# The first feed-forward unit split in two, and first blocks loaded in 1 KB runs from two queues

## The chip, the cores and the metric

The kernel runs on one NeuronCore of a Trainium2 chip. The metric is the device time of one execution, in microseconds (us). Before the change it is 294.58 us, the median of three runs (294.3 to 295.22). The profile is one execution recorded by the hardware profiler, with a span of 293.9 us.

Five engines work side by side, each on its own instruction queue: TensorE (PE, matrix products, with PEld for loading its stationary operand), VectorE (DVE), ScalarE (ACT), GpSimd (POOL) and SyncE (SP, which only issues transfers). Sixteen DMA engines move data. SP, ScalarE and GpSimd can start transfers.

## The reference

There are 4 batches, 8 heads, 768 rows and 64 columns per head. Attention is causal and restricted: keys form chunks of 32 rows, and each query attends to at most six chunks, chosen by an upper bound on its scores.

```python
ub = np.sum(np.maximum(q * k_min, q * k_max), axis=-1)     # per query and chunk
top_chunks = np.argsort(ub, axis=-1)[..., -top_k:]         # top_k = 6
scores = scale * np.matmul(q, k.transpose(0, 1, 3, 2))
mask = sel & (pos[:, None] >= pos[None, :])
attn = softmax(where(mask, scores, -1e9)); x = attn @ v
```

Then a gated feed-forward runs over all 3072 rows, with the heads side by side as 512 columns:

```python
gate = 1.0 / (1.0 + np.exp(-(x @ w_gate)))     # w_gate, w_val: 512 x 1536
val = x @ w_val
return gate * val @ w_out                      # w_out: 1536 x 512
```

The first 128 rows of a batch see only four chunks, so nothing is chosen for them: plain causal attention is enough.

## The kernel before, in words

The rows are cut into blocks of 128. A *first block* is block 0 of a batch; batches are numbered 0 to 3. Blocks are grouped into *units* of three blocks (384 rows), and each unit goes through the feed-forward together. Unit 0 holds the first blocks of batches 0, 1 and 2. Unit 2 holds two blocks of batch 0 and the first block of batch 3. The other six units hold three ordinary blocks each.

*First blocks* (`first`, L807 and on). SP loads k and q in two halves of four heads each (L742) and v whole (L737). The descriptors are runs of 64 numbers, 256 bytes, since a row of one head is 64 numbers. PE turns k and q (tiles kfT, qfT, L815) with four transposes of 128x128 each against a 32-bit identity, and they are cast to 16 bits (kf, qf). Then come scores (scf, L852), exponentials on ScalarE (attf, L857), the causal mask on GpSimd (L859), the product with v (pvf, L866), the division by the sum (rzf L872, xf L874), and the turn back (xpsf, L881) into xT, the input of the feed-forward. For batch 0 alone the keys of the first block are also kept in hk and their chunk minima and maxima in kcr, for later queries.

*Ordinary units.* For each, keys and queries are turned (`keys_wide`, `queries_wide`, tiles kn, kT, kt, qn, qT, qf, for units 1 and 2; `keys_blocks`, `turn_queries`, for later batches, on VectorE), the bounds are computed on PE with 32-bit operands (ub, L1002) and chunks are chosen on VectorE (`choose`: ubn, mx, ap, apt). Chosen chunks are encoded in the unused half of hq and hk, so that one product gives masked scores (`attend`: sc L1063, att L1074, mask L1080, pv L1096, x L1115, xps L1123).

*Feed-forward* (`ffn`, L1131 and on). For each of 12 parts of 128 hidden columns: four products for the gate (g, L1146), tanh on ScalarE (gate, L1154), four products for the value (v, L1146), and their combination on VectorE (hg, L1158). Then 12 products for each 128 rows (o, L1168), scaled (osb, L1177) and stored by SP (L1180). The tile name v_u is the value product; wg, wv and wo are the weights.

*Weights* are loaded by GpSimd with a cast from 32 to 16 bits, each of the three matrices in three transfers (L718, L719, L724). wg and wv are each cut by hidden columns; a third serves four parts of the feed-forward.

*Order.* The program lists operations with engines they may run on, estimated durations, priorities and dependencies. A planner (`Plan.walk`) walks through time and picks for each engine the ready operation of best priority. The priorities are shifted by the table NUDGES, and the assumed landings of transfers come from LANDS. The result is a fixed order for every engine; on the chip each instruction then waits only for what it needs. Buffers come from pools of fixed size, chosen by the planner ("np", "hg", "xt", "qm", "ubn" and others).

The loads of first blocks 0 to 2 come first on SP, then k and q of unit 1 (kq_u), then v. The first block of batch 3 is loaded and treated in the middle of unit 2. Weight transfers 2 and 3 and wo wait in the order for the masks of batch 2's first block.

The softmax here doesn't subtract the row's maximum and nothing guards it: scores larger than these inputs give would overflow.

## Time and profile before

| | |
|---|---|
| median of three runs | 294.58 us |
| span of the profile | 293.9 us |
| PE busy | 278.2 us, 95% |
| ACT, DVE, POOL busy | 195.8, 189.2, 92.5 us |
| bytes moved by DMA | 32.69 MB in 123233 packets, 111424 of them under 512 B |
| SP issue of a first-block transfer | 0.5 us |
| first transposes of first block 0, 1, 2 | 4.95, 7.86, 10.18 to 13.24 us |

The page gives busy time by engine, then the span in 40 slices with the tenths of each slice that an engine is busy, the clock granted to TensorE and the rate of transfers. Views of the trace list instructions in order of time, the wait before each and what ended it, and the busy time of engines in chosen stretches. Successive PE instructions overlap at their ends, so their pace is read from start to start. The chain of work that ended last goes from the transfers of q through those of wo (9% of the span) to PE, which makes up 78% of it.

### The profile page before, as it was taken

To read this page: it belongs to the slowest core of one execution; us is meant where nothing else is said; L and a number is where in the kernel's file an instruction comes from. 1 tells how busy PE (TensorE), PEld (TensorE's weight loads), DVE (VectorE), ACT (ScalarE), POOL (GpSimd) and SP (SyncE) were. 2 spreads that over 40 slices of the span, in tenths; PEclk is the share of its full clock that TensorE was granted. 3 is DMA by queue.
4 is the path that set the end of the run, shared out by engine and by line. 5 is a ranking of instruction groups with operands and counts; after the bars stand their busy time and mean duration, and the time that the engine had idled before them with its cause. 6 is when DMAs were issued, how large, how long until landed. Compare 5 with 4: busy or idle time off the path is not lost.

```text
span 293.9 us, 6954 instructions
## 1 busy us (share of the span) xinstructions
PE 278.2 (95%) x2656; PEld 176.7 (60%) x2656; DVE 189.2 (64%) x560; ACT 195.8 (67%) x398; POOL 92.5 (31%) x162
## 2 busy tenths in 40 slices
PE   2879998999989999999999999999999999999994
PEld 2645555767664566556666667676565557655651
DVE  8375883996999289999999899654134124432420
ACT  7674757977984879458889898886563466323321
POOL 6681314933652337013326954213000011000000
PEclk9977999999999999999999999999999999999999
DMA  7999999999967999399997300001100110011002
GB/s 165 218 249 216 197 197 235 220 146 166 184 100 90 203 188 184 67 215 152 142 210 145 111 3 3 0 2 39 71 2 1 50 60 0 2 38 71 0 15 95
DMA packets 123233, 32.69 MB, mean 111 GB/s; under 512 B 111424, under 2 KB 120128, under 8 KB 123200
## 3 DMA queue, kind: packets, MB, share of 16 engines
q1 hardware_dynamic: 118448, 27.53, 53.1%
q0 software_dynamic: 4752, 4.72, 9.5%
q8 instruction: 21, 0.34, 0.5%
q14 instruction: 12, 0.10, 0.1%
HBM read 30.67 MB, written 6.29 MB: 126 GB/s over the span
## 4 chain that ended last, share of the span: by engine, by line
PE 78%; DMA 10%; DVE 4%; SPq 2%; POOL 2%; ACT 1%; issue 1%; ACTq 0%; DVEq 0%
PE o_u L1168 20%; PE v_u L1146 18%; PE g_u L1146 18%; PE sc_u L1063 11%; DMA wo<-in_moe_w_out_dram 9%; PE pv_u L1096 6%; PE ube_u L1002 2%; SPq L742 2%; PE xps_u L1123 2%; DMA qf<-in_q_dram 1%; DVE qf_u L969 1%; DVE kcr L787 1%; DVE kt L953 1%; ACT attf L857 1%; PE qfT L815 1%
## 5 line engine op out<-in xcount | busy, mean ns | idle before, releaser
L1074 ACT ACTIVATE att_u<-sc_u 128x512 f16<-128x512 f32 (+3 forms) x184 | 88.0, 549 | 13.9 <-PE sc_u L1063 13.1
L1158 DVE SCALAR_TENSOR_TENSOR hg_u<-gate_u,v_u 128x384 f16<-128x384 f16 x96 | 51.8, 544 | 53.8 <-PE v_u L1146 37.0
L1146 PE MATMUL g_u<-xT_u,wg 128*128 128x384 f16 x384 | 79.3, 330 | 0.0
L1146 PE MATMUL v_u<-xT_u,wv 128*128 128x384 f16 x384 | 78.8, 328 | 0.3 <-DMA wv<-in_moe_w_val_dram 0.3
L1154 ACT ACTIVATE gate_u<-g_u 128x384 f16<-128x384 f32 x96 | 47.6, 495 | 39.1 <-DVE hg_u L1158 21.5
L1168 PE MATMUL o_u<-wo,hg_u 128*128 128x512 f16 x288 | 68.0, 379 | 1.1 <-DMA wo<-in_moe_w_out_dram 1.1
L1080 POOL TENSOR_SCALAR_AFFINE_SELECT att_u<-att_u 128x384 f16<-128x384 f16 (+1 forms) x56 | 28.4, 512 | 99.0 <-ACT att_u L1074 98.2
L1146 PEld LDWEIGHTS <-wv 128*128 128x128 f16 x384 | 36.8, 98 | 23.5 <-issue 0.8
L1146 PEld LDWEIGHTS <-wg 128*128 128x128 f16 x384 | 36.5, 99 | 21.8 <-issue 1.5
L1168 PEld LDWEIGHTS <-hg_u 128*128 128x128 f16 x288 | 27.1, 98 | 28.7 <-issue 1.5
L1177 ACT ACTIVATE osb_u<-o_u 128x512 f32<-128x512 f32 x20 | 12.1, 603 | 26.7 <-PE o_u L1168 25.0
L1096 PEld LDWEIGHTS <-att_u 128*128 128x128 f16 x640 | 25.5, 98 | 4.7
L1096 PE MATMUL pv_u<-v,att_u 128*128 128x65 f16 x640 | 28.0, 193 | 0.0
L1063 PE MATMUL sc_u<-hqo,hko 128*128 128x128 f16 (+2 forms) x220 | 27.8, 243 | 0.1
L1063 PE MATMUL sc_u<-hqe,hke 128*128 128x128 f16 (+2 forms) x220 | 27.1, 243 | 0.2 <-ACT att_u L1074 0.2
L1063 PEld LDWEIGHTS <-hke 128*128 128x128 f16 x220 | 16.8, 98 | 5.7 <-issue 1.2
L779 POOL CAST v<-v 128x512 f16<-128x512 f32 x23 | 13.9, 619 | 19.2 <-DMA v<-in_v_dram 18.9
L1063 PEld LDWEIGHTS <-hko 128*128 128x128 f16 x220 | 16.3, 98 | 4.8 <-issue 0.2
L576 DVE COPY xT_u<-xps_u 128x384 f16<-128x384 f16 (+1 forms) x17 | 5.7, 338 | 14.4 <-PE xps_u L1123 14.3
L1115 DVE TENSOR_TENSOR x_u<-pv_u,rz_u 128x384 f16<-128x384 f32 (+1 forms) x28 | 14.5, 523 | 0.4
L1025 DVE MAX8 mx_u<-ubn_u 128x8 f32<-128x8 f32 (+16 forms) x152 | 12.4, 156 | 0.1
L787 DVE TRANSPOSE_TENSOR_REDUCE kcr<-k 128x24 f32<-128x768 f32 x12 | 11.2, 941 | 0.8 <-DMA k<-in_k_dram 0.8
(119 smaller groups left out, 306.9 us busy)
## 6 DMA issues: line engine op xcount, KB each, us to landing
out_dram<-osb_u SPq DMA_DIRECT2D x24, 256.0 KB, 2.4
v<-in_v_dram SPq DMA_DIRECT2D x23, 256.0 KB, 5.0
k<-in_k_dram SPq DMA_DIRECT2D x12, 384.0 KB, 6.1
q<-in_q_dram SPq DMA_DIRECT2D x12, 384.0 KB, 6.8
wg<-in_moe_w_gate_dram POOLq DMA_DIRECT2D x3, 512.0 KB, 10.2
wv<-in_moe_w_val_dram POOLq DMA_DIRECT2D x3, 512.0 KB, 12.8
wo<-in_moe_w_out_dram POOLq DMA_DIRECT2D x3, 512.0 KB, 23.3
kf<-in_k_dram SPq DMA_DIRECT2D x8, 128.0 KB, 3.6
```

Source lines behind the costliest of these rows:

```text
L779: plan.add(f"v16_{b}_{ib}", {POOL: pool(H * D)}, lambda e: nc.gpsimd.tensor_copy(v16[b % 2][:, ib, :, 0:D], at(t)), reads=[t], writes=[("v ...
L787: plan.add(f"kx{m}_{name}_{p}", {DVE: dve(size)}, lambda e, m=m, op=op: nc.vector.tensor_reduce(out=outs[m](), in_=src(), op=op, axis=AX.X ...
L1025: nc.vector.max(at(mx)[:, e_, j, :], at(ubn)[:, e_, j, 0:max(8, u.seen[j])])
L1063: nc.tensor.matmul(at(t)[:, o:o + 128 * m], hk[b % 2][e_][:, p, 128 * jb:128 * jb + 128], hq[u.side][e_][:, p, 128 * x:128 * (x + m)], sta ...
L1074: plan.add(f"exp_{u.name}_{h}_{y}", {ACT: act(n)}, lambda e, t=t, att=att, b0=b0, n=n: nc.scalar.activation(at(att)[:, b0:b0 + n], at(t), ...
L1080: nc.gpsimd.affine_select(out=dv, in_=dv, compare_op=ALU.is_ge, fill=0.0, base=0, pattern=[[0, u.m], [1, 128]], channel_multiplier=-1)
L1096: nc.tensor.matmul(at(pv)[:, last, x, :], at(att)[:, c:c + 128], v16[b % 2][:, jb, h, :], start=(jb == 0), stop=(jb == ib))
L1115: plan.add(f"x_{u.name}_{p}", {DVE: dve(u.t)}, lambda e: nc.vector.tensor_tensor(at(x_).rearrange("p a (e d) -> p e a d", e=2), at(pv)[:, ...
L1146: nc.tensor.matmul(at(t), w16[:, c, 128 * fb:128 * fb + 128], at(u.xt)[:, c, :], start=(c == 0), stop=(c == 3))
L1154: plan.add(f"tanh_{u.name}_{fb}", {ACT: act(T)}, lambda e, g=g, gate=gate: nc.scalar.activation(at(gate), at(g), AF.Tanh, scale=0.5), read ...
L1158: plan.add(f"hg_{u.name}_{fb}", {DVE: dve(T)}, lambda e, w_=w_, gate=gate, hg=hg: nc.vector.scalar_tensor_tensor(at(hg), at(gate), 1.0, at ...
L1168: nc.tensor.matmul(at(o), at(hgs[fc])[:, 128 * tb:128 * tb + 128], wo16[:, fc, :], start=(fc == 0), stop=(fc == NFB - 1))
```

## The change

Five things change together.

1. Unit 0 keeps only the first blocks of batches 0 and 1 (256 rows). A new unit 8, also of 256 rows, holds the first blocks of batches 2 and 3. Unit 2 becomes 256 rows. Both feed-forwards of the start do four gate products before their first four value products. The weights are still cut in three, but keyed by hidden part.
2. k and q of first blocks are read as runs of four rows, 1 KB, which puts four rows of a head on one partition. All four blocks are loaded at the start; k by SP, q by ScalarE, v by either. Turning them takes eight ordinary 32-bit products of 64 outputs instead of four transposes, and the cast puts rows back in order.
3. Unneeded space is lent: 16-bit k and q, the exponentials and v of first blocks live in parts of hk, hq and v16 that come into use later; these later uses wait for the products pvf.
4. Products of the identity with itself (warm) are added at places where PE is expected idle, to keep its clock up.
5. The order is planned anew, with a table HOLDS that gives some operations an earliest time. ubn shares the buffer of qm.

The core of the diff:

```diff
-        Unit(0, [], [(0, 0), (1, 1), (2, 2)]),
+        Unit(0, [], [(0, 0), (1, 1)]),
-        Unit(2, [(0, 4), (0, 5)], [(3, 2)]),
+        Unit(2, [(0, 4), (0, 5)]),
+        Unit(8, [], [(2, 0), (3, 1)]),
...
-                for e_ in range(2):
-                    plan.add(f"{n}f{e_}_{b}", {SP: (450, 450)}, lambda e, t=t[n], src=src, e_=e_: nc.sync.dma_start(
-                        at(t).rearrange("s (p e) d -> s e p d", e=2)[:, e_], heads(src, b, e_)[:, 0:128].rearrange("p s d -> s p d")),
-                        writes=[(t[n], e_)], prio=prio + 0.1 * j, dma=(1125 if (b, n, e_) == (0, "k", 1) else 575, 256))
+                for g in range(2):
+                    plan.add(f"{n}f{g}_{b}", {(SP, ACT)[j]: (530, 530)}, lambda e, view=view, src=src, g=g: issue(e).dma_start(
+                        view()[:, 256 * g:256 * g + 256], heads(src, b, g)[:, 0:128].rearrange("p (s r) d -> s p (r d)", r=4)),
+                        writes=[keys[g]], prio=prio + 0.1 * j, dma=(400, 1024))
...
-                for p in range(NP):
-                    nc.tensor.transpose(at(t)[:, p], at(raw[n])[:, 2 * p:2 * p + 2].rearrange("s e d -> s (e d)"), ident32)
+                for r in range(4):
+                    for g in range(2):
+                        c = 256 * g + 64 * r
+                        nc.tensor.matmul(at(t)[ROWS[g], r].rearrange("d s p -> d (s p)"), raw[n][0]()[:, c:c + 64], ident32,
+                                         start=True, stop=True)
...
+    warm = ps("warm", "wm", [128, 128])
+    for name, n in {"": 8, "kfT_0": 2, "qfT_0": 3, "kfT_1": 3, "qfT_1": 3, "scf_1": 3, "kfT_2": 3, "qfT_2": 3, "scf_2": 3, "pvf_2_0": 3}.items():
+        for i in range(n):
+            op = plan.add(f"warm{name}_{i}", pe(213, 170), lambda e: nc.tensor.matmul(at(warm), ident32, ident32, start=True, stop=True),
...
+    for b in range(4):
+        first(units[b // 2 * 8], b, b % 2, raw_f[b], -3.0 + 0.5 * b)
...
+        first_ = 4 if u.i in (0, 8) else 1
+        for fb in range(first_):
+            gated(fb)
+        for fb in range(first_):
+            valued(fb)
...
     ffn(units[0], 1.0, 0.95)
+    ffn(units[8], 1.02, 0.95)
...
-    first(units[2], 3, 2, raw_f[3], 2.0)
```

In the order that results, PE has 34 warm products, 21 of them before the first value product of unit 0 and 13 after. ScalarE issues its ten transfers before its table load and its first copy. GpSimd issues the nine weight transfers among the masks of the first blocks.

## The prediction

> **What bounds the kernel now.** I began with the page: busy time per engine and the span in 40 slices of 7.35 us.
>
> ```profile
> PE 278.2 (95%) x2656; PEld 176.7 (60%) x2656; DVE 189.2 (64%) x560; ACT 195.8 (67%) x398; POOL 92.5 (31%) x162
> ...
> PE   2879998999989999999999999999999999999994
> ...
> PEclk9977999999999999999999999999999999999999
> DMA  7999999999967999399997300001100110011002
> ```
>
> TensorE is full from the fourth slice to the end; what it lacks lies in the first seven slices, where the transfer engines are full too, and in the last (the final eviction and store, untouched here). Next, stretches of that start, and of 70 to 100 us (columns: length, busy time with counts of PE, PEld, DVE, ACT, POOL, clock, transfer share, GB/s):
>
> ```profile
> 0.00:4.00 4.00, 0.00 (x0) 0.00 (x0) 2.76 (x8) 2.19 (x2) 3.03 (x10) 1.00 0.45 101
> ...
> 12.00:16.00 4.00, 3.79 (x44) 2.76 (x42) 2.16 (x8) 3.07 (x7) 2.23 (x4) 1.00 1.23 215
> 16.00:20.00 4.00, 2.68 (x23) 1.85 (x22) 3.49 (x13) 2.70 (x6) 3.50 (x6) 0.81 1.18 237
> 20.00:24.00 4.00, 3.33 (x14) 1.85 (x12) 2.33 (x5) 2.78 (x7) 2.90 (x4) 0.50 1.17 269
> ...
> 44.00:48.00 4.00, 2.98 (x25) 1.83 (x24) 0.73 (x2) 3.36 (x9) 1.85 (x4) 1.00 1.10 248
> ...
> 70.00:100.00 30.00, 28.93 (x296) 18.48 (x295) 25.07 (x72) 24.06 (x49) 14.24 (x24) 1.00 0.96 142
> ```
>
> Then TensorE in order of time (start, length, what):
>
> ```profile
> 13.24 1.10 PE L815 MATMUL kfT<-ident,kf 128*128 128x128 f32 x4
> ...
> 21.61 1.49 PE L1146 MATMUL g_u<-xT_u,wg 128*128 128x384 f16 x4
> 22.89 1.49 PE L1146 MATMUL v_u<-xT_u,wv 128*128 128x384 f16 x4
> 24.17 1.38 PE L1146 MATMUL g_u<-xT_u,wg 128*128 128x384 f16 x4
> 25.39 0.81 PE L1146 MATMUL v_u<-xT_u,wv 128*128 128x384 f16 x4
> ...
> 31.29 0.82 PE L1146 MATMUL v_u<-xT_u,wv 128*128 128x384 f16 x4 [0.31 <-DMA wv<-in_moe_w_val_dram]
> ...
> 48.09 1.89 PE L1168 MATMUL o_u<-wo,hg_u 128*128 128x512 f16 x8 [1.12 <-DMA wo<-in_moe_w_out_dram]
> ...
> 60.64 0.60 PE L815 MATMUL kfT<-ident,kf 128*128 128x128 f32 x4
> ```
>
> The first product of the first feed-forward starts at 21.61. Start to start, its groups of four take 1.28, 1.28 and 1.22 us; later ones take 0.65. So the clock is low until about 25.4, and PE waits twice for weights (0.31 and 1.12). Weight landings follow from issue plus time to landing (minimum, median, maximum of three each):
>
> ```profile
> 10.14 0.92 POOL L718 DMA_DIRECT2D wg<-in_moe_w_gate_dram  x1
> ...
> 12.24 0.77 POOL L719 DMA_DIRECT2D wv<-in_moe_w_val_dram  x1
> ...
> 18.42 0.76 POOL L719 DMA_DIRECT2D wv<-in_moe_w_val_dram  x1
> ```
> ```profile
> DMA to landing us min/median/max: 10.0/12.8/18.1
> ```
>
> Taking the shorter time for the earlier issue, the second lands at 18.42 + 12.8 = 31.2, where PE's wait ends, so the reading holds. The first lands at 12.24 + 10.0 = 22.2; wg (8.2/10.2/15.4) at 18.3, 27.3, 34.6; wo (issued from 20.7, 20.7/23.3/25.9) at 41.4, 44.7, 48.0. Weights thus arrive every 3.3 to 3.9 us, with one gap of 5.1 after 22.2. Up to about 48 us the kernel is bound by the weight stream, with PE part idle and part at half clock; after it, by PE.
>
> **What the Trainium skill says.** "TensorE: Matmul & The Clock Gate", Part 1: the clock is halved by default and after about 3.4 us of little work. The 1.28 against 0.65 agrees. Its Part 4 says that transpose-mode work doesn't count as busy for this; kfT at 13.24 still takes 1.10 against 0.60 late, in a stretch with PE 95% busy, so the trace agrees. "DMA: Bandwidth & Descriptors", Specifications, puts full rate at 512 B and above. The trace can only say that 256 B runs are slow: the three first blocks (9 x 256 KB = 2.36 MB, issued from 0.81, last transpose of them at 13.24) need about 11 us, some 215 GB/s; it has no 1 KB loads. The same page, "Issuing engines are not separate DMA queues": a second queue saves issue time only. An issue takes 0.5 us on SP here, and the transfer share is above 1 from 4 us on, so I price the second queue at nothing.
>
> **The change, part by part.** I count PE work at full clock, with steps read start to start: 0.65 for four 128x384, 0.437 for four 128x256 (one 128x256 score to the next instruction is 0.11), 0.056 for a 128x128 f16, 0.030 for a 128x65, 0.11 for an f32 transpose (after the four kfT at 60.64 the next instruction starts at 61.08).
>
> *First-block loads.* Four blocks are now loaded ahead of the weights instead of three: twelve arrays of 256 KB instead of nine, eight of them in 1 KB runs. If these cost what 256 B ones do, this adds 3 x 262 KB / 215 GB/s = 3.7 us; if they run at the best rate of any stretch I read (269 GB/s), 8 x 0.98 + 4 x 1.22 = 12.7 against 11.0, +1.7. Who pays? The weights are queued by GpSimd after one mask of block 0, near 10 us as before, and SP's three v loads at 16.73 are held 17.8 us in its queue while weights land every 3.3 to 3.9 us: beside weights it is the short-run loads that give way. So I take wv at 22.2 again; bounds 21 (the gap closed) and 24.5 (most of the 3.7 passed on).
>
> *Turning.* 1 KB runs need eight ordinary f32 products of 64 outputs per k or q instead of four transposes. Trace of before for ordinary narrow f32 products:
>
> ```profile
> 36.47 0.45 PE L1002 MATMUL ube_u<-qf_u,kcr 64*32 64x320 f32 x1
> ...
> 36.77 0.43 PE L1002 MATMUL ube_u<-qf_u,kcr 64*32 64x320 f32 x1
> ```
>
> Eight of these side by side take about 0.27 us for 320 columns, so 0.107 for 128 columns. If two 64-wide ones run together: 4 x 0.107 = 0.43 a turn; one after another: 0.86; with the four passes that the skill's "FP8 and Floating Point Precision", TensorE Precision Notes, gives for true f32 (4 x 0.053), one after another: 1.71. I take 0.86, so eight turns cost 6.9 instead of 3.5: +3.3, all before the weights land. They are ordinary products, and six fill-in products go ahead of them, so the clock should be full by about 10 us.
>
> *PE work before the first v group.* Before: 6 turns 2.64, three blocks' scores, values and turns back 1.34 + 0.72 + 0.67, three kT 0.99, one g group 0.65: 7.0 us. After, by the instruction order: 8 turns 6.9, 1.79 + 0.96 + 0.78, two kT 0.66, four g groups 1.75: 12.8 us. It must fit between about 4 and 22 us; it does if the chain of masks keeps up. GpSimd must put nine weight issues (0.77 each) and eight masks (0.62) through by about 21 us, as it did nine and six by 22.9. ScalarE has ten issues (0.5) and a table load (1.28) before its first copy, ready near 7.4 instead of 2.1; I cost the delay at nothing, since its first input turned up at 6.07 before and block 1 isn't needed until 18.
>
> *PE work after it.* The whole rises by 3.3 (turns) + 0.24 (288 products of 256 instead of 192 of 384, 2.5 ns more for each of 96) = 3.5. So what remains after the first v group changes by 3.5 - (12.8 - 7.0) = -2.2 us.
>
> *Clock and waits.* The first v starts on wv's landing, 22.3, not 22.89 behind a half-speed g: -0.6. The v and g at half speed took 2.50 instead of 1.30: -1.2. The wv wait goes (-0.3), because the first third of the weights now serves 16 groups of 0.437 and eight kT and qT turns. The output products of the first unit come about 21 us of work behind the first v, near 22.3 + 21 + 2.8 (fill-ins, below) = 46, when the wo part that comes first is in (41.4 at the latest, if nothing slips) and the next ones are needed at 49 or later: -1.1.
>
> *Fill-in products.* 34 in all, 13 of them after the first v group: 13 x 0.213 = 2.8 with four passes (1.4 if two do). They are put where PE was expected idle, so I charge +2.8 whole, for the product or for the idleness under it.
>
> *At no cost:* extra buffers, the borrowed tiles, ubn in qm's buffer and the added order constraints: all act on vector and scalar work under the PE stream; and hg and gate at width 256 add about 36 x 0.41 - 24 x 0.544 = 1.7 us of DVE, less than block 3's DVE work (about 2.5) that leaves the crowded stretch after 60.
>
> Sum: -2.2 - 0.6 - 1.2 - 0.3 - 1.1 + 2.8 = -2.6; 294.58 - 2.6 = 292.0 us.
>
> **Rivals.** *A: given back later.* In 70 to 100 us DVE is 84% busy, and PE idles 1.07. If preparing unit 3 can't follow a PE that comes 2.6 us sooner, the lead is lost as new waits there: 294.3. Against it: k and q of batch 1 load earlier, with block 3 out of that place. *B: slower.* Turns cost 1.71 and the start is bound by PE, or the late ScalarE or GpSimd holds the fourth block back; 6.8 us more PE work in 18 us that hold 12.8, partly at half clock, starts the v groups some 4 us late: 296.0 (292.0 + 4). For it: every engine is over two thirds busy in 16 to 20. Against it: the narrow products above. *C: more.* The fill-ins sit in gaps that cost nothing further, and the rest holds: -5.4, 289.2.
>
> **Chances.** Forecast (290.3 to 293.6) 0.57, A 0.19, B 0.17, C 0.07. Faster by over 0.3% (below 293.70) holds the forecast, C and a third of A: 0.70; within 0.3% most of A: 0.13; slower 0.17, B. The range 290.2 to 295.6 leaves out C's end and most of B.
>
> **What would show it.** First g group near 18.5 to 20 and first v near 22.3, groups of 0.44 from the start; a clock near 1.0 in 16 to 28; turns of about 0.9; no PE wait for wo; block 3 turned before 20. The forecast is wrong if wv lands after 24, turns take over 1.2, or PE idles over 2 us between 60 and 100.

## The result and the profile after

The changed kernel takes 297.87 us (median, 297.53 to 298.10), the kernel before 294.90 beside it: ratio 1.0102, 95% interval 1.0079 to 1.0124, so slower by 1%, where 292.0 was forecast. In a second series (kernel e6) the ratio was 1.0050 (1.0028 to 1.0072). All four executions of the first series had a mean granted clock of 0.994 or less; in the second, nine of the eighteen that its ratio counts had 0.999 or more. The page of the changed kernel, for the rows shown of before:

```profile
PE 285.2 (96%) x2916; PEld 197.7 (67%) x2916; DVE 190.6 (64%) x581; ACT 193.1 (65%) x405; POOL 94.7 (32%) x164
...
PE   5599999999999999999999999999999999999994
...
PEclk9779999999999999999999999999999999999998
DMA  6999999974979999999990110001100011011002
```

TensorE is full from the third slice on instead of the fourth, but it is busy for 7.0 us longer in all, and the low clock has moved forward by one slice. The stretches (columns as before):

```profile
4.00:8.00 4.00, 2.31 (x38) 2.02 (x39) 0.69 (x1) 0.00 (x0) 0.10 (x1) 1.00 0.93 286
8.00:12.00 4.00, 0.87 (x16) 0.63 (x12) 0.00 (x0) 1.51 (x2) 0.00 (x0) 0.93 1.07 276
12.00:16.00 4.00, 3.59 (x38) 3.40 (x40) 2.04 (x10) 2.47 (x5) 2.94 (x4) 0.50 1.18 286
16.00:20.00 4.00, 4.00 (x46) 3.16 (x44) 1.38 (x2) 1.65 (x4) 3.74 (x7) 0.72 1.12 239
...
70.00:100.00 30.00, 30.00 (x301) 19.54 (x299) 28.16 (x77) 25.79 (x51) 15.05 (x25) 1.00 0.95 161
```

TensorE works 0.87 of the 4 us from 8 to 12, and then runs at half clock. From 70 to 100 it never waits. So nothing is given back there; the loss is at the start. TensorE there, in order of time:

```profile
6.96 1.92 PE L915 MATMUL kfT<-ident,kf 128*64 128x128 f32 x32
12.41 0.61 PE L959 MATMUL scf<-hke 64*128 64x128 f16 x8 [3.53 <-ACT hke L652]
12.95 1.97 PE L915 MATMUL qfT<-ident,qf 128*64 128x128 f32 x16
...
21.65 1.09 PE L915 MATMUL qfT<-ident,kqvf 128*64 128x128 f32 x16
...
24.81 1.36 PE L1327 MATMUL warm<-ident 128*128 128x128 f32 x10
...
27.75 0.60 PE L1257 MATMUL g_u<-xT_u,wg 128*128 128x256 f16 x4
...
30.25 0.60 PE L1257 MATMUL v_u<-xT_u,wv 128*128 128x256 f16 x4
```

The first keys are turned by 8.88, then TensorE stands 3.53 us until ScalarE has cast them. The first value product starts at 30.25 instead of 22.89: 7.36 us later. From it to the end of the span it is 296.4 - 30.25 = 266.15 us, against 293.9 - 22.89 = 271.0: 4.9 us shorter. Together they make the +2.5 us of span. ScalarE, where the wait points:

```profile
0.80 2.20 ACTq L840 DMA_DIRECT2D qf<-in_q_dram  x3
3.03 1.28 ACTq L840 DMA_DIRECT2D kqvf<-in_q_dram  x2
6.01 0.54 ACTq L840 DMA_DIRECT2D qf<-in_q_dram  x1
...
9.79 0.66 ACTq L840 DMA_DIRECT2D kqvf<-in_q_dram  x1
10.47 1.28 ACT L652 ACT_TABLE_LOAD   x1 [10.47 <-DMA kqvf<-in_q_dram]
11.77 1.07 ACT L652 CAST hke<-kfT 128x512 f16<-128x512 f32 x2
```

Ten issues of about 0.65 us are 6.6 us of work, yet the last starts at 9.79, with gaps from 4.31 to 6.01 and from 8.6 to 9.79. The program as built says why. In it the loads of SP and ScalarE share eight completion counters in turn, and an issue that takes a counter again waits for the landing of the load that used it last (the number is the counter waited for):

```
ScalarE, in order: q, q, q, q (no wait), q (counter 0), q (2), q (4), v (5), v (0), q (3), table load, first cast
```

Counter 3 belongs to block 0's values, issued by SP at 5.56. The chain of waits shows it:

```profile
1.49 4.05 DMA kf<-in_k_dram
...
5.56 4.21 DMA vf<-in_v_dram
...
9.79 0.66 ACTq L840
...
10.47 1.28 ACT L652
...
11.77 0.59 ACT hke L652
...
12.41 0.61 PE scf L959 x8
```

ScalarE's last issue waits until the values have landed (9.77), and everything that ScalarE computes is queued behind it. GpSimd's mask needs ScalarE's exponentials, and in its order the weights come after that mask:

```profile
13.79 0.64 POOL L967 TENSOR_SCALAR_AFFINE_SELECT attf<-attf 128x512 f16<-128x512 f16 x1 [0.64 <-ACT attf L965]
14.38 1.00 POOL L803 DMA_DIRECT2D wg<-in_moe_w_gate_dram  x1
15.37 0.77 POOL L803 DMA_DIRECT2D wv<-in_moe_w_val_dram  x1
```
```profile
DMA to landing us min/median/max: 11.8/15.0/16.8
```

The first wv lands at 15.37 + 11.8 = 27.2, not 22.2. TensorE waits for no weights in the changed kernel, since it comes later still.

### The profile page after: what moved, and what is told of

Its sections match the earlier page's. It is cut to its first block, busy times and chain, and to the rows that moved or that the text cites. A ratio compares the mean times of both kernels' runs of the same rounds, so it can differ in the third digit from the quotient of the medians.

```text
span 296.4 us, 7538 instructions
## 1 busy us (share of the span) xinstructions
PE 285.2 (96%) x2916; PEld 197.7 (67%) x2916; DVE 190.6 (64%) x581; ACT 193.1 (65%) x405; POOL 94.7 (32%) x164
## 4 chain that ended last, share of the span: by engine, by line
PE 94%; DMA 3%; ACT 1%; DVE 0%; ACTq 0%; issue 0%; SPq 0%
PE g_u L1257 21%; PE v_u L1257 21%; PE o_u L1296 21%; PE sc_u L1177 12%; PE pv_u L1210 7%; PE ube_u L1116 3%; PE warm L1327 2%; PE qfT L915 2%; PE xps_u L1237 2%; DMA vf<-in_v_dram 1%; DMA kf<-in_k_dram 1%; PE kfT L915 1%; PE kT_u L1009 1%; PE qT_u L1009 1%; PE scf L959 1%; ACT L652 0%
## 5 line engine op out<-in xcount | busy, mean ns | idle before, releaser
L1188 ACT ACTIVATE att_u<-sc_u 128x512 f16<-128x512 f32 (+3 forms) x184 | 89.5, 546 | 22.2 <-PE sc_u L1177 21.5
L1277 DVE SCALAR_TENSOR_TENSOR hg_u<-gate_u,v_u 128x384 f16<-128x384 f16 (+1 forms) x108 | 53.2, 501 | 46.6 <-PE v_u L1257 34.4
L1257 PE MATMUL g_u<-xT_u,wg 128*128 128x384 f16 (+1 forms) x432 | 79.9, 308 | 0.0
L1257 PE MATMUL v_u<-xT_u,wv 128*128 128x384 f16 (+1 forms) x432 | 79.5, 308 | 0.0
L1270 ACT ACTIVATE gate_u<-g_u 128x384 f16<-128x384 f32 (+1 forms) x108 | 49.4, 461 | 30.3 <-DVE hg_u L1277 17.4
L1257 PEld LDWEIGHTS <-wg 128*128 128x128 f16 x432 | 40.8, 98 | 18.0 <-issue 0.5
L1257 PEld LDWEIGHTS <-wv 128*128 128x128 f16 x432 | 41.2, 98 | 17.3
L1296 PEld LDWEIGHTS <-hg_u 128*128 128x128 f16 x288 | 26.8, 98 | 26.6 <-issue 0.6
L1305 ACT ACTIVATE osb_u<-o_u 128x512 f32<-128x512 f32 x22 | 13.2, 599 | 24.9 <-PE o_u L1296 22.9
L1210 PE MATMUL pv_u<-v,att_u 128*128 128x65 f16 x640 | 27.1, 193 | 0.0
L1227 DVE RECIPROCAL rz_u<-pv_u 128x6 f32<-128x6 f32 (+1 forms) x28 | 5.0, 181 | 16.7 <-PE pv_u L1210 16.5
L1229 DVE TENSOR_TENSOR x_u<-pv_u,rz_u 128x384 f16<-128x384 f32 (+1 forms) x28 | 14.7, 527 | 0.4
L1327 PE MATMUL warm<-ident 128*128 128x128 f32 x68 | 12.2, 313 | 1.4 <-POOL ident masks.py:199 1.4
L885 DVE TRANSPOSE_TENSOR_REDUCE kx<-k 128x24 f32<-128x768 f32 x12 | 11.3, 948 | 3.3 <-DMA k<-in_k_dram 3.3
```

Of the source, the lines that this page charges most:

```text
L1188: plan.add(f"exp_{u.name}_{h}_{y}", {ACT: act(n)}, lambda e, t=t, att=att, b0=b0, n=n: nc.scalar.activation(at(att)[:, b0:b0 + n], at(t), ...
L1210: nc.tensor.matmul(at(pv)[:, last, x, :], at(att)[:, c:c + 128], v16[b % 2][:, jb, h, :], start=(jb == 0), stop=(jb == ib))
L1229: plan.add(f"x_{u.name}_{p}", {DVE: dve(u.t)}, lambda e: nc.vector.tensor_tensor(at(x_).rearrange("p a (e d) -> p e a d", e=2), at(pv)[:, ...
L1257: nc.tensor.matmul(at(t), w16[:, c, 128 * fb:128 * fb + 128], at(u.xt)[:, c, :], start=(c == 0), stop=(c == 3))
L1270: plan.add(f"tanh_{u.name}_{fb}", {ACT: act(u.rows)}, lambda e: nc.scalar.activation(at(gate), at(g), AF.Tanh, scale=0.5), reads=[g], writ ...
L1277: plan.add(f"hg_{u.name}_{fb}", {DVE: dve(u.rows)}, lambda e: nc.vector.scalar_tensor_tensor(at(hg), at(gate), 1.0, at(w_), ALU.add, ALU.m ...
```

## The experiments

Theory T1: ScalarE's waiting issues hold its first cast back, and with it TensorE's clock and the weights. R1: the narrow turns bind the start. R2: the fill-in products alone are the loss. T2 (weights that start before the loads hold these back) and T3 (the bytes ahead of the weights bind) came up on the way. "First scores" is where TensorE first has cast keys; every span is of the profiled execution, every median is over all executions. The kernels e5 and e17 are one program, and so are the changed kernel and e6. There is no e3.

| kernel | first scores | first weight issue | first value product | span | span less first value product | median | ratio to before |
|---|---|---|---|---|---|---|---|
| before | 8.9 | 10.1 | 22.9 | 293.9 | 271.0 | 294.90 | 1 |
| changed | 12.4 | 14.4 | 30.2 | 296.4 | 266.2 | 297.87 | 1.0102 |
| e6 changed, again | 13.1 | 15.1 | 30.5 | 296.7 | 266.2 | 296.81 | 1.0050 |
| e1 loads all on SP | 9.3 | 11.2 | 39.7 | 305.5 | 265.8 | 307.31 | 1.0409 |
| e2 no fill-ins | 12.0 | 13.8 | 26.5 | 291.7 | 265.2 | 293.85 | 0.9969 |
| e4 fill-ins in the pause | 14.0 | 15.7 | 29.1 | 295.3 | 266.2 | 296.88 | 1.0042 |
| e5 ScalarE issues three | 8.7 | 10.6 | 36.7 | 302.6 | 265.9 | two speeds | |
| e17 the same again | 10.6 | 12.5 | 27.1 | 293.0 | 265.9 | two speeds | |
| e7 three, weights late | 10.7 | 15.1 | 28.9 | 294.8 | 265.9 | 295.87 | 1.0008 |
| e8 and no fill-ins | 10.0 | 14.4 | 27.6 | 292.5 | 264.9 | 295.15 | 1.0006 |
| e9 weights at 4 us | 22.3 | 4.0 | 39.8 | 306.0 | 266.2 | 307.98 | 1.0420 |
| e10 three, weights spaced | 10.6 | 14.6 | 27.6 | 293.5 | 265.9 | 295.23 | 0.9994 |
| e11 and no fill-ins | 10.8 | 14.7 | 27.6 | 293.3 | 265.7 | 294.86 | 0.9972 |
| e12 e11 less block 3 | 8.6 | 12.6 | 24.4 | 289.3 | 264.9 | 291.39 | 0.9875 |
| e13 e2 less block 3 | 10.6 | 12.5 | 24.6 | 289.4 | 264.8 | 291.22 | 0.9845 |
| e14 e2, weights at 10.7 | 12.5 | 10.7 | 27.6 | 293.1 | 265.5 | 294.32 | 0.9962 |
| e15 fill-ins, weights at 10.8 | 13.4 | 10.8 | 30.1 | 296.2 | 266.1 | 296.46 | 1.0038 |
| e16 e2, weights at 12.8 | 12.3 | 12.8 | 27.5 | 292.6 | 265.1 | 294.09 | 0.9961 |
| e18 e14, 8 fill-ins in the pause | 11.9 | 10.7 | 25.45 | 290.9 | 265.4 | 293.24 | 0.9935 |
| e19 e2, 8 fill-ins in the pause | 12.2 | 14.0 | 26.8 | 292.0 | 265.2 | 293.89 | 0.9964 |

The column before the last two is the main finding: in all nineteen profiles of the changed kernel and its variants the span is the first value product plus 264.8 to 266.2 us. What comes after it always takes about 5 to 6 us less than before, part of it because the change moves work ahead of that product (5.8 us in the prediction's count). The question is only when that product starts. Apart from the queues and the fill-ins, no run takes one of the five changes out by itself, so their shares in the 5 to 6 us are not shown.

**e1: all loads on SP.**

```diff
-        return nc.scalar if e == ACT else nc.sync
+        return nc.sync
```

> The changed kernel with one edit: all twenty first-block loads are issued by SyncE; order, 1 KB runs, split and fill-in products stay. Theory T1 (ScalarE's own compute is queued behind its load issues, each of which may have to wait for an earlier transfer to land: first cast 11.77 us after the start, where 7.4 was forecast): the first cast moves to 8.5 to 10 us (one queue issues more slowly, about 0.55 us each, so the last piece of the first keys lands later than 5.54), the pause of TensorE between 8.9 and 12.4 us shrinks below 1.5 us, the clock in 12 to 20 us rises from 0.5-0.7 to above 0.85, first value product at 25 to 27 us instead of 30.25, time 293 to 295.5. Rival R1 (the narrow turns in float32 bind the start): no change, 297 to 298.5. Rival R2 (the fill-in products alone are the loss): 297 to 298.5. A queue count that matters for the transfers themselves would show as a lower GB/s in 4 to 12 us and a slower kernel.

Measured 307.31: a miss. The first cast came at 7.83, as T1 wants, and the time rose by 3.5%. On one engine the issues follow each other every 0.64 us, so the twentieth would come near 13; but the weights, now free at 11.2, went out ahead of the last three loads, and an issue then took up to 2.64 us:

```profile
11.75 2.64 SPq L840 DMA_DIRECT2D kqvf<-in_k_dram  x1
...
15.52 0.65 SPq L835 DMA_DIRECT2D kqvf<-in_v_dram  x1
```

One of these loads took 13.2 us to land, and TensorE stood 6.2 us for keys. The rate of transfers was lower too, as the expectation asks of a queue count that matters. From 4 to 8 us the two kernels that issue from SP alone show (before, then e1; the changed kernel is above):

```profile
4.00:8.00 4.00, 2.08 (x9) 1.74 (x10) 3.96 (x8) 3.82 (x5) 2.14 (x6) 1.00 1.20 237
```
```profile
4.00:8.00 4.00, 2.58 (x34) 1.80 (x33) 0.69 (x1) 0.17 (x1) 0.09 (x1) 1.00 0.71 203
```

In e1 the transfer engines are not full (share 0.71, against 1.20 before). A load of 128 KB every 0.645 us makes 203 GB/s by estimate, just what was moved: here the issuing engine is the limit. So the second queue is worth something (last load issued at 9.8 instead of 15.5), and a second mechanism is at work.

**e5 and e17: ScalarE issues three loads, SP the rest.**

```diff
+    given = []
+
     def issue(e):
-        return nc.scalar if e == ACT else nc.sync
+        given.append(e)
+        return nc.scalar if e == ACT and given.count(ACT) <= 3 else nc.sync
```

> The changed kernel with one edit: ScalarE issues only its first three loads, before any issue that has to wait; the other seven go to SyncE. T1: activation table loaded near 4 us, first cast near 8 us when the first keys are turned (the pause of TensorE before the first scores under 1 us), first mask of GpSimd near 10 us instead of 13.8, first value weights landed near 23 us instead of 27.2, first value product at 23.5 to 26, clock about 1.0 from 8 us on, time 291 to 294: the forecast of 292 with its failed step mended. R1 and R2: 297 to 298.5.

The first cast came at 7.96, close to the 7.4 of the forecast, and the first scores at 8.72. But this kernel has two speeds: of 20 executions 13 took 293.4 to 295.3 us and 7 took 302.2 to 306.1. A profile of the second kind, in views of GpSimd, of the transfers of a tile, of waits for it, and of the queues' shares of the transfer engines from 12 to 24 us:

```profile
10.64 0.99 POOL L803 DMA_DIRECT2D wg<-in_moe_w_gate_dram  x1
```
```profile
L838 SPq DMA_DIRECT2D kqvf<-in_v_dram x2: 592/592/593, 9.7 to 12.5; - x2
...
  ACT hko L652: 10.4, 1
...
DMA to landing us min/median/max: 3.3/4.3/13.4
```
```profile
q0 software_dynamic: 1693, 1.69, 86.6%
q1 hardware_dynamic: 2136, 0.75, 32.3%
```

The weights (q0) went out at 10.64, before the last first-block load (12.5). They took 86.6% of the engines' span, SP's queue 32.3%, and the load needed 13.4 us to land, where 3.4 to 6.5 were seen in the changed kernel. ScalarE stood 10.4 us on it, and with it all the rest. e17 has a profile of the other kind:

> The two-speed kernel again (ScalarE issues three loads), for a look at the other speed: 294.6 or 304. Theory: the speed is set by whether the first weight piece goes out before the last first-block load (12.5 us). In the slow executions TensorE turned the first queries at full speed (1.09 us), the first mask came at 10.05 and the weights at 10.6. In a fast execution the first turns should be at half speed (1.98 us, as in the kernels with the weights held back), the first mask near 11.5 to 12 us, the weights from 12 to 12.6 us, and no load should take over 8 us to land before 15 us.

```profile
11.92 0.64 POOL L970 TENSOR_SCALAR_AFFINE_SELECT attf<-attf 128x512 f16<-128x512 f16 x1 [0.92 <-ACT attf L968]
12.51 1.00 POOL L803 DMA_DIRECT2D wg<-in_moe_w_gate_dram  x1
```

As expected: the first turn took 1.98 us (5.89) instead of 1.09 (5.95 in e5), so the mask and the weights came 1.9 us later, behind the last load (11.9). No first-block load took over 5.4 us, and the first value product started at 27.1. So a start of the weights 1.9 us sooner or later flips this kernel by 9 us. Why the first turn differs is open: the granted clock is recorded as 1.00 in both. The two speeds aren't sharp either: of the 18 executions of e17 seven took 293.7 to 297.2 us and eleven 298.4 to 307.0, with three between the groups (297.2, 298.4, 300.5) that no profile shows.

**e9: weights at once.** The sharpest test of T2, that weights which start before the loads hold these back. The first three pieces, with the second gate piece ahead, go before GpSimd's first copy.

```diff
+    ops = plan.order()
+    for name in ("wg4", "wv0", "wg0"):
+        op = next(o for o in ops if o.name == name)
+        ops.remove(op)
+        ops.insert(next(i for i, o in enumerate(ops) if o.name == "hkf1"), op)
...
```

> The changed kernel with one edit: GpSimd issues the first three weight pieces before its first copy, so from about 4 us instead of 14.4 us; loads on both queues stay as they are. Theory T2 (weights that start before the first-block loads are out hold these back): the loads issued after 5 us land 8 to 14 us after their issue instead of 3.4 to 6.5, TensorE stands still for over 5 us between 8 and 24 us though the first weights land near 12 to 14 us, time 302 or more. If the weights and the loads shared the engines without harm, the time would fall by the 4 to 7 us by which the weights come sooner: 291 to 294.

Measured 307.98. The chain of waits holds both mechanisms in three lines:

```profile
1.49 4.11 DMA kf<-in_k_dram
5.62 14.14 DMA vf<-in_v_dram
19.78 0.55 ACTq L840
```

Block 0's values, issued at 5.62 in the middle of the weights, took 14.14 us instead of 4.21, and ScalarE's last issue waited for them. The first scores came at 22.3. The Trainium skill, "DMA: Bandwidth & Descriptors", Queues, rings and completion order, says that each engine alternates between queues packet by packet. The shares are in line with that, though no run isolates it: from 8 to 20 us the weights' queue had 77.9%, those of SP and ScalarE 23.3% and 14.9%.

**e6: the changed kernel again**, as a base.

> The changed kernel itself once more, as the base for the three kernels measured with it: 297.5 to 298.5, first cast near 11.8 us, last first-block load issued near 9.8 us, first weight piece near 14.4 us, first value product near 30.

Measured 296.81, below what was expected (296.46 without one execution of 761 us and one of 299.2, which the ratio leaves out). Those with a mean clock of 0.999 or more took 294.7 to 296.2, those at 0.994 or less 296.8 to 299.0. The mean clock suggests that the half clock after the pause is not in every execution; where it is, it costs some 2 us. Much of the distance between the two series (1.0102 and 1.0050) fits this mix.

**e4: the clock alone.**

```diff
+        if op.name == "scf_0":
+            for _ in range(14):
+                nc.tensor.matmul(at(warm), ident32, ident32, start=True, stop=True)
         op.emit(op.engine)
```

> The changed kernel with 14 more fill-in products put before the first scores, where TensorE stands still from 8.88 to 12.41 us; 14 x 0.213 = 3.0 us at full clock, so they fit the pause. Nothing else moves. It isolates the clock's share of the late cast. T1: clock 12 to 18 us at 1.0 instead of 0.5-0.7, turns of the third and fourth block near 1.05 us instead of 1.6 to 1.97, first value product 2.5 to 3.3 us earlier, time 294.5 to 295.5. If the clock costs nothing there: 297.5 to 298.5.

Measured 296.88, less gain than expected, because the added products overshot:

```profile
10.66 3.39 PE L1424 MATMUL warm<-ident 128*128 128x128 f32 x28
13.99 0.40 PE L959 MATMUL scf<-hke 64*128 64x128 f16 x8
...
29.15 0.60 PE L1257 MATMUL v_u<-xT_u,wv 128*128 128x256 f16 x4
```

Fourteen took 0.24 us each and put the scores at 13.99 instead of 12.41. From scores to first value product it is 15.16 us, against 17.84 in the changed kernel: the half clock there costs 2.7 us (2.3 for e6 and 1.5 for e15, which has the same work, in the same way). The pause before the scores and their length (0.40 at full clock, 0.61 at half) tell when it falls: pauses of 1.26, 1.74 and 1.98 us kept it (e18, e16, e2), 2.34, 2.60, 3.53 and 4.21 lost it (e14, e15, changed, e6). The pause is longest where the first turn took 1.09 us (changed, e6); in e2, e14, e15 and e16 it took 1.98, which brings the end of the turns nearer to the cast.

**e2: no fill-ins.**

```diff
+        if op.name.startswith("warm") and not op.name.startswith("warm_"):
+            continue
         op.emit(op.engine)
```

> The changed kernel without its 28 fill-in products (idle products of the identity that only keep TensorE awake) after the first eight; both queues stay. Nothing of the result depends on them. T1: the late first cast stays at 11.8 us; TensorE no longer carries about 28 x 0.213 = 6.0 us of fill-in at full clock, but where they filled real gaps the gap comes back, and the clock may stay low for longer: 293 to 296. R2 (they alone are the loss): below 292.5. If they pay for themselves by the clock: 297.5 or slower.

Measured 293.85, ratio 0.9969 (0.9948 to 0.9990): faster than before, if barely. It is 4.0 us below the first series of the changed kernel, but that is not the price of the fill-ins: set against e6 among executions of like mean clock it is 2.3 us (0.997 or more in e2, 0.999 or more in e6) or 2.8 us (0.994 or less). R2 in the form that was tested (below 292.5) is not borne out; that taking out the fill-ins alone turns slower into faster stays true. TensorE now meets the weights:

```profile
26.46 0.61 PE L1257 MATMUL v_u<-xT_u,wv 128*128 128x256 f16 x4 [0.70 <-DMA wv<-in_moe_w_val_dram]
```

R1 as the whole cause falls here, since with the eight narrow turns in place TensorE still waits. What narrow turns cost against four transposes no run tests; they stay part of the sequence that binds the changed kernel (e15, below).

**e7, e8, e10, e11: ScalarE issues three, and the weights are held until the loads are out** (by order in e7 and e8, by three repeated copies on GpSimd in e10 and e11; e8 and e11 without fill-ins). The edits of e7 and of e10 on top of that of e5:

```diff
+        if op.name in ("wg0", "wv0", "wg4"):
+            held.append(op)
+            continue
+        if op.name == "wv4":
+            for o in held:
+                o.emit(o.engine)
...
+        if op.name == "wg0":
+            for _ in range(3):
+                named["hkf1"].emit(named["hkf1"].engine)
```

> Two edits of the changed kernel: ScalarE issues only three loads (as in the run before, which had two speeds, 294.6 and 304), and GpSimd issues the first three weight pieces behind three more masks, directly ahead of the fourth piece. In the slow executions of the run before, the weights went out from 10.6 us, two us before the last first-block load (12.5), and that load took 13.4 us to land; ScalarE's cast stood 10.4 us on it. Theory T2 (two needs: ScalarE free early, and the first-block loads out before the weights): weights from 13 to 14 us, last first-block load lands within 5 us, no pause of TensorE over 2 us between 12 and 28 us, one speed only, first value product at 24 to 27 us, time 291.5 to 294.5. If the two speeds have another cause: they stay, 294 and 304. R1 (narrow turns): 297 to 298.5.

> The kernel of the run before this one (ScalarE issues three loads, weights behind three more masks) and without the 28 fill-in products after the first eight. If the late first cast and the fill-ins are separate losses, both gains add: 288.5 to 291, about 4 us under the kernel without fill-ins alone (293.85). If they are one loss seen twice (without fill-ins TensorE only waits for the weights, which land every 3.4 us): 293 to 294.5.

> ScalarE issues three loads, as in the two-speed kernel, and GpSimd repeats one copy of block 0's keys three times (0.73 us each, same values) ahead of the first weight piece, so that the weights start near 12.8 us: just behind the last first-block load (issued at 12.5) and not, as in the kernel with weights behind three masks, at 15.2. Theory T2: one speed; the last block load lands within 6 us; first value weights land at 24.5 to 26 us (28.9 with weights at 15.2, 27.2 in the changed kernel, 21.8 where they started at 10.6), time 293 to 295, 1 to 2 us below the changed kernel. If starting weights two us later makes no difference: two speeds, 294.6 and 304.

> The kernel of the run before this one without the 28 fill-in products. T2 with the fill-ins as a separate loss: 290.5 to 293. If TensorE then only waits for weights: as that run, within 1 us.

The part of T2 on the loads holds: no execution over 299.4 us, and no first-block load took over 5.0 us to land. The gains missed. The weights went out at 14.4 to 15.1, no sooner than in the changed kernel, because masks or copies delayed them more than meant, and TensorE waited for the first wv, from 0.2 us in e10 to 1.6 in e8. Taking the fill-ins out then gains only 0.4 to 0.7 us. Two things go against it: the fill-ins seem in part to have stood in for that wait, and without them the clock falls more often (15 of 20 executions of e8 had a mean clock of 0.994 or less, 2 of 20 of e7).

**e12 and e13: the fourth block's first loads left out** (its tile set to zero, so that block's output rows are not computed from its data).

```diff
+        if op.name in ("kf0_3", "kf1_3", "qf0_3", "qf1_3", "vf_3"):
+            if op.name in ("kf0_3", "qf0_3", "vf_3"):
+                nc.gpsimd.memset(raw_f[3][op.name[0]][0](), 0.0)
+            continue
```

> The kernel of the run before this one with the fourth block's first loads left out (keys, queries and values of block 0 of batch 3, 5 transfers, 0.79 MB of reads; GpSimd sets the tile to zero instead, so the output rows of that block are not the reference's). It prices the transfer of the fourth block, which the forecast counted at nothing for the weights. If the start is bound by the bytes that have to pass before the first value weights (theory T3): 0.79 MB at the 250 GB/s of 8 to 16 us is 3.1 us, so the weights land 2 to 3 us sooner and the time falls by 1.5 to 3 us against the run before. If the moment of issue binds, not the bytes: under 0.7 us.

> The changed kernel (both queues as they are) without the 28 fill-in products and without the fourth block's first loads (set to zero on GpSimd; the output rows of that block are not the reference's), to be set against the kernel without fill-ins, 293.85 us. ScalarE has three transfers fewer to issue (7 instead of 10), so its first cast also comes sooner, near 10 us. T3 (bytes): first value weights land near 24 instead of 26.5 us, time 291 to 292.5. If the wait is elsewhere: 293 to 294.

Measured 291.39 and 291.22, 3.5 and 2.6 us below e11 and e2. T3 fits, but not as bytes alone. In e12 the weights went out 2.2 us sooner and wv took 10.3 us instead of 11.8 to land; in e13 1.2 us sooner and 11.0 instead of 11.7. So of the sooner landing 0.7 to 1.5 us are the transfer itself, and the rest is an earlier issue. With four executions each, none of them at a low mean clock, and in e12 the faster first turn, these gains are no clean price of the bytes.

**e14, e15, e16: only the issue of the first two weight pieces moves**, behind idle selections on GpSimd (nine in e14 and e15, twelve in e16). wg0 and wv0 are moved as in e9, and:

```diff
+        if op.name == "wg0":
+            nc.gpsimd.memset(wo16[:, 0], 0.0)
+            for _ in range(9):
+                nc.gpsimd.affine_select(out=wo16[:, 0], in_=wo16[:, 0], ...)
```

> The changed kernel without the 28 fill-in products, and with the first two weight pieces moved ahead of GpSimd's first copy, behind ten idle selections on a tile that the output weights overwrite later (about 0.6 us each), so that they go out near 10 us instead of 13.8, just behind the last first-block load (9.4 to 9.8). If the moment of issue binds: first value weights land near 22 to 23.5 us instead of 26.5, first value product near 23 to 24, time 290.5 to 292.5. If the transfers only share the engines with the loads still in flight (the first-block loads land until 15 us) and these come later: first value product no sooner than 25.5 us, 293 to 295. If they are held back as with weights from 4 us: over 300.

> The kernel of the run before this one with the fill-in products kept: the changed kernel with nothing but the earlier first two weight pieces. If TensorE's own work binds up to the first value product in the changed kernel (it never waits after 12.4 us), earlier weights bring nothing: 297 to 298.5, or less by the clock alone (295.5 with the full clock). If the weights' landing binds: as much gain as the run before has over the kernel without fill-ins.

> As e14 with the first two weight pieces out near 11.8 us, half way between 10 and the 13.8 of the kernel without fill-ins (293.85). If the moment of issue binds, half the gain of e14: 292 to 293; if there is a best moment between the loads and the weights, this is the lowest of the three.

e15 settles that weights don't bind the changed kernel: issued 3.6 us sooner, with the first wv in at 23.5, they leave its first value product at 30.1:

```profile
30.05 0.60 PE L1257 MATMUL v_u<-xT_u,wv 128*128 128x256 f16 x4
```

It is bound by TensorE's own sequence: the pause, then turns and fill-ins, in part at half clock. Without fill-ins (e14) it came at 27.6 in a profile with the half clock, above what was expected; executions with a clock of 0.997 or more took 292.4 to 293.5 us, those below 293.8 to 296.8. e16 took 294.09, above its 292 to 293. The medians of e2, e16 and e14 (293.85, 294.09, 294.32) show no gain from sooner weights; only among executions at 0.997 or more is there one (293.5, 293.1 and 292.5, each at the median of these). At 10.7 us the weights do no harm, as both queues have issued their loads by 9.8.

**e18 and e19: the parts together.** No late fill-ins (the edit of e2), eight in the pause (that of e4 with `range(8)`); in e18 also the sooner weights (that of e14).

> The kernel with the first two weight pieces out at 10.7 us and without the 28 late fill-in products, with 8 fill-in products put ahead of the first scores, where TensorE stands 2 to 4 us (8 x 0.24 = 1.9 us). The clock then stays at 1.0 in every execution; the first scores come near 12.4 us; from there the work to the first value product took 15.2 us at full clock with 4.0 us of fill-in in it, so 11.2, plus about 1.5 us of waits for VectorE: first value product near 25 us, behind its weights at 23. Span 25 + 265.3 = 290.3, time 291.5 to 292.5 in nearly all executions, faster than both kernels.

> The changed kernel without the 28 late fill-in products and with the same 8 fill-ins ahead of the first scores; weights where they are (from 13.8 us). If the weights' landing is the second bound: first value product at 26.4 to 27 us with its weights, 0.7 to 1.5 us above the run before this one, time 292.8 to 294, most of them with full clock. If both kernels are alike within 0.3 us, the weights do not bind.

e18 takes 293.24, ratio 0.9935 (0.9912 to 0.9958), faster than both kernels, if by less than expected:

```profile
11.87 0.40 PE L959 MATMUL scf<-hke 64*128 64x128 f16 x8 [1.26 <-ACT hke L652]
...
25.45 0.60 PE L1257 MATMUL v_u<-xT_u,wv 128*128 128x256 f16 x4
```

e19 lies 0.65 us above it at 293.89, and its first value product waits 0.86 us for wv. The intervals of the two ratios overlap, so that difference isn't settled by the times, only by the wait. The eight fill-ins do keep the clock (8 of 9 executions of e18 and 19 of 22 of e19 had 0.996 or more, 11 of 20 in e2), but e19's median is no lower than e2's 293.85: they steady the time more than they shorten it.

## Why the prediction was wrong

The forecast of 292.0 meant a span of 293.9 - 2.6 = 291.3, with the first value product at 22.3 and 269.0 us after it. Measured: 30.25 and 266.15. The first term is 7.95 us too low, the second 2.85 too high. (In its own figures 3.5 - 5.8 is -2.3, not -2.2; this changes nothing.)

- **The step that failed** is this one: "ScalarE has ten issues (0.5) and a table load (1.28) before its first copy, ready near 7.4 instead of 2.1; I cost the delay at nothing". It counted issues as 0.5 us of work and not as instructions that may wait. The first cast came at 11.77, 4.4 us later than the 7.4: 2.9 us are the two gaps in which an issue waits, and some 1.6 the ten issues at 0.66 us each. Its input was there before 8.88. That mending this step alone brings the first scores to 8.72 is shown (e5). That it brings the time to 292 is not: in some executions the weights then go out too soon, and the others take 294.6 (median), only 1.1 us less than the executions of e6 at full clock (295.7). The neighbouring steps fell with it: "the clock should be full by about 10 us", "near 10 us as before" for the weights (14.4), wv at 22.2 (27.2).
- **The 7.95 us in parts, by estimate.** The first scores came at 12.41 against 8.72 where ScalarE issues three loads (e5): 3.7. The half clock: 17.84 - 15.16 = 2.7 (e4; 1.5 to 2.7 over the profiles). The fill-ins ahead of the first value product: 15.16 against 13.58 us from scores to product in e18, 1.6 (e15 against e14, both with a fall of the clock: 1.5). Together 8.0. The forecast had the late cast at nothing, booked 1.2 us for a clock that would be full, and had all fill-ins behind the product. The parts are differences between several runs, so the close sum is in part luck, and no run has all of them: with the scores at 8.72 the weights leave before the loads (e5), and e18, which mends the other two, still starts the product at 25.45.
- **The second queue at nothing** was wrong on both sides. It brings the last load's issue from 15.5 to 9.8 (e1), and costs ScalarE's start. The ground given, a transfer share above 1 from 4 us on, was that of the 256-byte runs; with 1 KB runs from one queue the share is 0.71 and the issues bind (e1). The Trainium skill, "DMA: Bandwidth & Descriptors", Issuing engines are not separate DMA queues, says that several issuing engines save only issue time, usually small beside the transfer; issue time is what is saved here too, but twenty issues of 0.65 us are 13 us.
- **Who pays for the fourth block.** "Beside weights it is the short-run loads that give way" was right, and stronger than thought: 13.4 and 14.1 us to land in e5 and e9, where 3.4 to 6.5 were seen in the changed kernel. But these loads stand ahead of everything in the engines' fixed order, so their giving way costs 9 us and more (e5, e9). Early weights were no gift.
- **Turns** took 0.93 to 1.02 us at full clock (in e18 from 12.19 to 13.12 and from 16.64 to 17.66), forecast 0.86: about 1 us more for eight, so the choice among 0.43, 0.86 and 1.71 was right. At half clock the step is 1.76 (12.95 to 14.71 in the changed kernel). The prediction reads the slow kfT at 13.24 as a mark of transposes; in the same trace the ordinary scores at 12.49 took the 0.61 us of the half clock, so this trace doesn't tell the two kinds of work apart.
- **Fill-ins**: 2.8 charged for thirteen, all behind the first value product. e15 less e14, which differ in the 28 alone, is 2.1 us in the medians, and 2.6 to 2.8 among executions of like clock. The total was near, in part by luck; the place was not: 1.5 to 1.6 lie ahead of the product, which the forecast had at nothing.
- **Right**: the half-speed g and v at 24 us, the wv wait and the wo wait are gone; TensorE waits for nothing from 24 us to the last output products (282 us). The rest fell by 4.9 us, not 2.0, mainly because the fill-ins there cost 0.6 (266.1 against 265.5, e15 and e14) and not 2.8. The remainder of about 0.7 isn't traced.
- **The rivals.** A (given back at 70 to 100 us) fell: 30.00 of 30 us busy. B named "the late ScalarE or GpSimd" with a first value product some 4 us late and 296.0. It came nearest, but it was the first block's cast that was late and not the fourth block, and its 4 us were 8; that its time lies so near to the 296.81 of the second series is luck, as the 4.9 us after the product make up for it. C (289.2) had the fill-ins in gaps that cost nothing. The stated sign "wrong if wv lands after 24" came true. Of the others, groups of 0.44 and no wait for wo were seen; the first g group came at 27.75, the clock in 16 to 20 us was 0.72, and the last turn of a first block began at 21.65, not before 20.

## What to carry to other kernels

Here ten loads issued by ScalarE held its own first cast back by waits that had nothing to do with it. When an engine that computes also issues loads, look for the counter that each issue waits on, and for what stands behind it. Before you move work earlier, ask what it starts: here an earlier cast starts the weights, and weights that start before the last load is issued hold it for some 13 us, while weights just behind it do no harm (e14, e18). Place fill-in products only in a measured pause: with 28 taken out and eight put there, +1.0% (+0.5% in the second series) became -0.36% (e19), and -0.65% with the weights sooner as well (e18).

## What was not expected of the hardware

- A queue of large weight transfers took 78 to 87% of the transfer engines' span beside the queues of the 256-byte and 1 KB loads (e9, e5); the time to land of block 0's values rose from 4.2 to 14.1 us (e9).
- The clock survived pauses of TensorE up to 1.98 us and fell after 2.34 us and more, in the profiles of seven runs. The Trainium skill, "TensorE: Matmul & The Clock Gate", Part 1, speaks of an idle window of about 3.4 us; here less was enough.
- Runs of 1 KB load the transfer engines less than runs of 256 bytes. From 4 to 8 us, before any weights, 237 GB/s took a share of 1.20 in the kernel before (all 256 bytes), 286 took 0.93 in the changed kernel and 203 took 0.71 in e1 (k and q in 1 KB runs). Per full share that is an estimated 198, 308 and 286 GB/s. The 1 KB runs give the room, and the second queue, by issuing sooner, fills it.
- The first turn of keys or queries took 1.09 us in some executions and 1.97 in others of the same program (e5, e17), at a recorded clock of 1.00. The longer one is just as long as a turn at a recorded 0.50 (12.95 in the changed kernel). In the kernel before, too, the first scores take the 0.61 us of the half clock at a recorded 1.00, and 0.40 later on:

```profile
8.88 0.61 PE L852 MATMUL scf<-qf,kf 64*128 64x128 f16 x8
...
15.20 0.40 PE L852 MATMUL scf<-qf,kf 64*128 64x128 f16 x8 [0.21 <-ACT xT_u L574]
```

So at the start of these profiles a recorded 1.00 is no sign of full pace. It seems that TensorE was still at half pace there; why some executions leave it sooner, no run settles.
